# Q and K sums copied into the operand buffers and transposed there, row buffers given up for half a V weight piece

## The chip, the cores and the metric

One core of one Trainium2 chip runs the whole program. The metric is the device time of one execution in microseconds (us); before the change the median of three runs is 1652.26 us (1645.23 to 1652.44).

## The reference

A memory-augmented attention A and a gated feed-forward network (FFN) B are mixed by a gate that is computed per row of x.

```
g = sigmoid((x * gate_w).sum(-1))
for s in range(64):                      # 64 segments of 32 rows, mem: 8 rows
    h = concat([mem, x[32*s : 32*s+32]]) # 40 rows, 640 wide
    q, k, v = h @ Wq, h @ Wk, h @ Wv     # 32 heads of 192 each
    p = softmax(mask(q @ k.T * 192**-0.5))
    o = (p @ v) @ Wo
    mem, a[s] = o[:8], o[8:]             # the next segment needs mem
b = (gelu(x @ w_gate) * (x @ w_up)) @ w_down
out = g * a + (1 - g) * b
```

The segments form a chain: the memory rows that one produces are input of the next. The last eight rows of a segment's 32 ("left" rows) need the memory of no later segment, so their Q, K and V can be made for four segments at once.

## The kernel before

**Stages.** First comes the FFN for all 2048 rows (into a scratch tensor), then the 64 segments one after the other. A segment treats the 32 heads as four octets of eight heads. Each of Q, K and V of an octet is a sum over five pieces of weights (k = 0 to 4, 128 x 1536 bf16, 384 KB each); a piece is four matmuls of 384 columns that stand side by side on 32 output columns each. The sums end in PSUM, ACT (ScalarE) copies each to SBUF, and for Q and K the DVE (VectorE) transposes 32 x 32 blocks of it into the buffers `Qs` and `Ks`, which the score matmuls read. POOL (GpSimd) copies the middle third of Q into `Qz`, in which half the partitions are zero.

**What sets the order.** The order is written out by hand in lists (`PROG`, `PROG1`, `PROG3`): `("g", n, k)` is piece k of group n of `GROUPS`, `tq`/`tk` the transposes of an octet, `sc` its scores, `ex` its softmax, `pt` the transposes of the probabilities, `pv` the product with V, `wo` the output projection, `lf`/`le` work on left rows that fills gaps. Segments 0, 1 and 2 of four follow `PROG` or `PROG1`, every fourth (called q = 3 below, the first three q = 0, 1, 2) `PROG3`. All engines take their instructions in the order in which this list adds them. Waits are worked out by a small scheduler in the same order: an operation waits for the last writer of what it reads, and for the last writer and all readers of what it overwrites.

**Places that matter below.** In `PROG` the last piece of group 3 (V of octet 2 and Q of octet 3) stands directly ahead of `("sc", 2)`. In `PROG3` the last piece of group 2 (V of octet 1, Q and K of octet 2) and one piece of group 3 stand ahead of `("sc", 1)`, and the last piece of group 3 ahead of `("sc", 2)`. The ACT copies of those sums (L1159 for Q and K, L1162 for V) are added with the last piece, so ahead of these scores. The copies go to `rows_sb[0]` (Q) and `rows_sb[1]` (K), 768 bytes per partition each, and the transposes (L1176) from there to `Qs` and `Ks`. Scores start with two matmuls that write the mask (L1187), then L1195, L234 and L1202.

**Weights that don't fit.** SBUF holds most pieces for good. Thirteen pieces of Q, K and V and three of Wo share their place with a partner, and are loaded anew in each segment by a DMA from SP's queue as soon as the matmuls of the piece in that place are done. One Q piece (k = 2 of the octet that comes last in one segment and first in the next) is copied to four blocks of 768 bytes (`ek_off`) late in each segment by POOL: blocks 0 and 1 to the row buffers in one copy (L1455) after `sc 3`, block 2 after it (L1459), block 3 to a V buffer after `pv 2` (L1459). The load of the piece's partner follows these copies. The blocks are read by the next segment's first Q, and by left-row matmuls (`LQ`, L930) that stand just behind `pv 3` (L1282 and L1284): there only where the left unit's octet is the one whose piece was copied, which is so for q = 0 and q = 1 in all but the last group of four segments.

**The end of a segment.** Half of the output sum goes through ACT (`half_copy`, L1345, one instruction) to SBUF, DVE adds the other half (`half_sums`, L1350), and further adds and transposes give the next segment's memory columns.

Of the kernel before, what the change touches and what calls it, by code (L numbers as in the profile page):

```python
# [238 lines left out]
def _build(nc, A_x, A_mem0, A_Wq, A_Wk, A_Wv, A_Wo, seg_len, w_gate, w_up, w_down,  # L239
# [65 lines left out]
    wsB["rows"] = al(2 * 768)  # L305
# [91 lines left out]
    rows_sb = [bview(wsB_off["rows"] + b * 768, 768) for b in range(2)]  # L397
    r_rows = [sreg(wsB_off["rows"] + b * 768, 768) for b in range(2)]
# [31 lines left out]
    U3h = [bview(wsB_off[nm], 768).rearrange("p (t c r) -> p t c r", c=3, r=64) for nm in ("Q", "p")]  # L430
    r_U3h = [sreg(wsB_off[nm], 768) for nm in ("Q", "p")]
    r_U3hp = [[[sreg(wsB_off[nm] + x + 4 * i, 4) for x in xs_] for i in range(3)] for nm, xs_ in (("Q", (0, 8)), ("p", (0, 256, 512)))]
    assert wsB["Q"] >= 768 and wsB_off["p"] + 768 <= wsB_off["K"]
# [7 lines left out]
    zp_off = [wsB_off["p"], wsB_off["Q"]]  # L441
    ek_off = [wsB_off["rows"], wsB_off["rows"] + 768, wsB_off["K"] + 24 * R - 768, wsB_off["v"]]
    assert zp_off[0] + 4 * DJ <= ek_off[2] and zp_off[0] % 64 == 0 and 4 * DJ <= wsB["Q"]
# [5 lines left out]
    zpart = [fview(x, DJ * 4) for x in zp_off]  # L449
    zsum = zpart[0]  # L450
    r_zp = [sreg(x, DJ * 4) for x in zp_off]
# [60 lines left out]

    def piece_src(key):
        if key[0] == 3:
            return Wo2[:, key[1]]
        m, o_, k = key
        return (Wq2, Wk2, Wv2)[m][:, k, OW * o_:OW * (o_ + 1)]

    def piece_size(key):
        return GO if key[0] == 3 else GQ  # L520

    def piece_view(key, o):
        if key[0] == 3:
            return bview(o, GO).rearrange("p (c n) -> p c n", n=Dm)
        return bview(o, GQ)
# [44 lines left out]
    def seg_order(s):  # L570
        keys = []
        for item in PROGS[s % 4]:
            if item[0] == "g":
                keys += [(m, octet(s, i), item[2]) for m, i in group_at(item)]
# [5 lines left out]
    assert len(orders[0]) == len(set(orders[0])) == 3 * KT * NOCT + NWP  # L580
# [17 lines left out]
    seq = lk + lv[2] + lw[NLW:] + lv[0] + lv[1] + lw[:NLW]  # L598
# [369 lines left out]
    def vl_mm(s, k):  # L968
        o, bk, b = octet(s, 0), lb["v"], s // 4 % 2
        g_, rg_ = unit_piece((2, o, k))  # L970
        S_.add("pe", [lambda e, j=j: e.matmul(  # L971
            ps[32 * j:32 * j + 32, bk, 0:384], XLg[b][:, k, :], g_[:, 384 * j:384 * (j + 1)], start=(k == 0), stop=(k == KT - 1),
            tile_position=(0, 32 * j)) for j in range(4)],
            reads=[rg_, r_XLg[b]], writes=[r_ps[bk]], name="Vl s%d o%d k%d" % (s, o, k))

    units = [(0, NOCT - 1)] + [(1, o) for o in LUNIT[3].values()] + [(0, 1), (0, 2), (0, 0)]
    for n, (g, o) in enumerate(units):
# [5 lines left out]
        for m in range(2):  # L983
            left_rows(g, o, m, LBK[m], lst[b][:, :, m], [r_lst[b]], rows_sb[m], r_rows[m])
# [131 lines left out]
    def proj(s, item):  # L1116
# [8 lines left out]
        def mms(m, bk, lhs, k, g_, keep):  # L1125
            fns = []
            for j in range(4):
# [4 lines left out]
                else:  # L1132
                    rhs = g_[:, 384 * j:384 * (j + 1)]
# [8 lines left out]
        for n, (m, i) in enumerate(group_at(item)):  # L1142
            o, bk = octet(s, i), bk_of[(m, i)]
            g_, rg_ = piece(s, (m, o, k))
            S_.add("pe", mms(m, bk, htile(k), k, g_, n > 0),
                   reads=([rg_] if rg_ else r_ek) + [r_Hm[int(k >= KA[1])], r_HxT], writes=[r_ps[bk]],
                   name="%s s%d o%d k%d" % ("QKV"[m], s, o, k))
        for m, i in ms:
            if m == 2 and s % 4 == 0 and i:
                o, bk = octet(s, i), bk_of[(3, i)]  # L1150
                g_, rg_ = piece_view((2, o, k), res_off[(2, o, k)]), r_res[(2, o, k)]
                S_.add("pe", mms(2, bk, XLg[s // 4 % 2][:, k, :], k, g_, False),
                       reads=[rg_, r_XLg[s // 4 % 2]], writes=[r_ps[bk]], name="Vl s%d o%d k%d" % (s, o, k))
        if k < KT - 1:
            return
        for m, i in ms:
            o, bk = octet(s, i), bk_of[(m, i)]
            if m < 2:
                S_.add("act", lambda e, m=m, bk=bk: e.activation(out=rows_sb[m], in_=ps[:, bk, 0:384], func=ACTF.Copy),  # L1159
                       reads=[r_ps[bk]], writes=[r_rows[m]], name="rows evac")  # L1160
# [13 lines left out]
    def row_transp(s, m, o):  # L1174
        dst, rd = ((Qs, r_Qm), (Ks, r_Km))[m]
        S_.add("dve", lambda e: e.transpose(out=dst[:, :, 0:L], in_=rows_sb[m].rearrange("p (c r) -> p c r", r=L)),  # L1176
               reads=[r_rows[m]], writes=[rd], name="T%s s%d o%d" % ("qk"[m], s, o))
# [92 lines left out]
    def pv_oct(s, o):  # L1270
# [33 lines left out]
        if o == NOCT - 2 and s + 1 < NSEG:  # L1304
            ek_copy(s, (3,))
# [371 lines left out]
```

## Time and profile before

| what | value |
|---|---|
| median of three runs | 1652.26 us (1645.23 to 1652.44) |
| the profiled execution, its own span | 2114.2 us |
| its granted TensorE clock, mean over the core | 0.654 |
| DMA bytes moved, mean rate | 499.28 MB, 236 GB/s |
| DVE, ACT, POOL busy | 1005.8, 792.9, 553.3 us |
| Q and K copies by ACT (L1159) | 512 of 491 ns |
| transposes to `Qs`, `Ks` by DVE (L1176) | 512 of 562 ns |

The profiled execution is longer than the timed runs; durations below are those of that execution. In the rows of groups the columns are line, engine, operation, what is written and read, shapes, and count, then busy time in us and the mean in ns of one, then the engine's idle time before them. In the rows of a timeline the columns are start and duration in us, engine, line and operation; matmul ends are modelled, so neighbouring matmuls overlap in it. A window's row has its length and the busy time of PE (TensorE), PEld (its weight loads), DVE, ACT and POOL, then the granted clock, the DMA engines' busy share and their rate in GB/s.

### The profile page before, as it was taken

The numbers are of one execution on the slowest core, as the hardware profiler recorded it, in microseconds if no ns is written. First come the engines' busy times: TensorE is split into PE (matmuls) and PEld (weight loads), VectorE is DVE, ScalarE is ACT, GpSimd is POOL, SyncE is SP. The second block draws the span as 40 slices with busy tenths as digits, with TensorE's granted clock in tenths as the row PEclk, the third lists the DMA queues.
The fourth block names the chain that finished last, engine by engine and source line by source line (L and its number), as shares of the span: only waits on it lengthen the run. The fifth ranks groups of instructions, "written<-read, shape, count | busy, mean of one in ns | idle before, by whom it ended". The sixth has DMA issues, their size and how long they took to land.

```text
span 2114.2 us, 75845 instructions
## 1 busy us (share of the span) xinstructions
PE 2098.0 (99%) x37107; PEld 958.1 (45%) x28147; DVE 1005.8 (48%) x3039; ACT 792.9 (38%) x1890; POOL 553.3 (26%) x1625
## 2 busy tenths in 40 slices
PE   9999999999999999999999999999999999999997
PEld 3444344444444444444444444444444444444444
DVE  4233254554545454545545454545455454545453
ACT  1111244343434343444434343434444343434342
POOL 1000023232232223232222323232322223222332
PEclk6666666666666666666666666666666666666666
DMA  9612577776768777677767677776777676777775
GB/s 319 182 33 57 184 268 260 248 270 232 253 219 275 244 258 241 227 255 254 274 233 249 221 268 249 255 251 225 248 256 270 239 258 212 261 256 249 254 264 174
DMA packets 275415, 499.28 MB, mean 236 GB/s; under 512 B 121119, under 2 KB 136327, under 8 KB 275079
## 3 DMA queue, kind: packets, MB, share of 16 engines
q1 hardware_dynamic: 271000, 491.30, 68.8%
q8 instruction: 255, 4.18, 0.8%
q10 hardware_dynamic: 4079, 3.14, 0.5%
q14 instruction: 81, 0.66, 0.1%
HBM read 473.25 MB, written 21.09 MB: 234 GB/s over the span
## 4 chain that ended last, share of the span: by engine, by line
PE 99%; DMA 0%; DVE 0%; SPq 0%; POOL 0%; ACT 0%; issue 0%; ACTq 0%; POOLq 0%; DVEq 0%
PE ps L226 26%; PE ps L1138 25%; PE ps L1338 9%; PE ps L1383 8%; PE ps L1282 4%; PE ps L930 4%; PE ps L839 4%; PE ps L836 4%; PE ps L862 3%; PE ps L1364 3%; PE ps L1187 2%; PE ps L1284 2%; PE ps L234 1%; PE ps L1195 1%; PE ps L971 1%; PE ps L1254 1%
## 5 line engine op out<-in xcount | busy, mean ns | idle before, releaser
L226 PE MATMUL ps<-arena 128*32 128x384 bf16 x8960 | 887.8, 430 | 0.4 <-ACT arena L1159 0.4
L1138 PE MATMUL ps<-arena 128*32 128x384 bf16 x8640 | 857.5, 420 | 2.0 <-DVE arena L1583 2.0
L1138 PEld LDWEIGHTS ps<-arena 128*32 128x32 bf16 x8640 | 303.3, 117 | 525.3 <-issue 379.7
L1176 DVE STREAM_TRANSPOSE arena<-arena 128x384 bf16<-128x384 bf16 x512 | 276.5, 562 | 144.1 <-ACT arena L1159 144.1
L1159 ACT ACTIVATE arena<-ps 128x384 bf16<-128x384 f32 x512 | 230.0, 491 | 160.1 <-PE ps L1138 160.1
L1214 DVE TENSOR_REDUCE arena<-ps 104x4 f32<-104x160 f32 x256 | 83.0, 324 | 340.2 <-PE ps L1202 340.2
L1338 PE MATMUL ps<-arena 128*32 128x320 bf16 x3456 | 241.0, 404 | 0.0
L1012 POOL COPY arena<-arena 128x96 bf16<-128x96 bf16 x256 | 70.2, 274 | 475.3 <-PE ps L1202 311.4
L1267 ACT ACTIVATE arena<-ps 128x448 bf16<-128x448 f32 x192 | 104.4, 544 | 237.7 <-PE ps L1254 233.3
L1179 POOL COPY arena<-arena 64x160 bf16<-64x160 bf16 x256 | 81.9, 320 | 385.5 <-DVE arena L1176 384.3
L1162 ACT ACTIVATE arena<-ps 128x384 bf16<-128x384 f32 x256 | 125.2, 489 | 128.1 <-PE ps L1138 127.5
L1383 PE MATMUL ps<-arena 128*64 128x320 bf16 x1536 | 169.6, 387 | 0.0
L1226 ACT ACTIVATE ps<-ps 104x160 f32<-104x160 f32 x256 | 74.8, 292 | 239.5 <-DVE ps L1216 239.5
L1320 ACT ACTIVATE arena<-ps 128x480 bf16<-128x480 f32 x192 | 109.5, 570 | 93.8 <-PE ps L1284 85.7
L930 PE MATMUL ps<-arena 128*32 128x384 bf16 x1280 | 142.5, 408 | 0.0
L1338 PEld LDWEIGHTS ps<-arena 128*32 128x32 bf16 x3456 | 113.3, 129 | 56.9 <-ACT arena L1261 18.1
L1282 PE MATMUL ps<-arena 128*64 128x160 bf16 x1536 | 135.2, 263 | 0.0
L1284 PE MATMUL ps<-arena 128*64 128x64 bf16 x1536 | 128.6, 225 | 0.0
L1228 DVE TENSOR_REDUCE arena<-ps 104x4 f32<-104x160 f32 x256 | 81.8, 319 | 88.4 <-ACT ps L1226 87.4
L1383 PEld LDWEIGHTS ps<-arena 128*64 128x64 bf16 x1536 | 93.2, 127 | 49.4 <-issue 9.6
L1282 PEld LDWEIGHTS ps<-arena 128*64 128x64 bf16 x1536 | 94.1, 126 | 42.8 <-ACT arena L1159 23.0
L1411 ACT ACTIVATE arena<-ps 128x384 bf16<-128x384 f32 x120 | 57.3, 491 | 123.9 <-DVE arena L1580 74.0
(102 smaller groups left out, 2518.2 us busy)
## 6 DMA issues: line engine op xcount, KB each, us to landing
arena<-in_A_Wk_dram SPq DMA_DIRECT2D x335, 384.0 KB, 5.8
arena<-in_A_Wv_dram SPq DMA_DIRECT2D x335, 384.0 KB, 8.4
arena<-in_A_Wo_dram SPq DMA_DIRECT2D x205, 480.0 KB, 4.3
arena<-in_A_Wq_dram SPq DMA_DIRECT2D x209, 384.0 KB, 4.8
arena<-left_qk_scratch SPq DMA_DIRECT2D x126, 96.0 KB, 3.9
left_qk_scratch<-arena SPq DMA_DIRECT2D x49, 192.0 KB, 4.6
left_qk_scratch<-arena SPq DMA_DIRECT2D x30, 96.0 KB, 3.7
ffn_b_scratch<-arena ACTq DMA_DIRECT2D x16, 160.0 KB, 2.3
```

Source lines behind the costliest of these rows:

```text
L226: return e.add_instruction(mybir.InstMatmult(name=nm, start_tensor_calc=like["start"], stop_tensor_calc=stop, tile_size=(128, 32), tile_po ...
L930: fns.append(lambda e, outp=outp, rhs=rhs, j=j: e.matmul(outp, lhs, rhs, start=(k == 0), stop=(k == KT - 1), tile_position=(0, 32 * j)))
L1138: fns.append(lambda e, outp=outp, rhs=rhs, j=j: e.matmul(outp, lhs, rhs, start=(k == 0), stop=(k == KT - 1), tile_position=(0, 32 * j)))
L1159: S_.add("act", lambda e, m=m, bk=bk: e.activation(out=rows_sb[m], in_=ps[:, bk, 0:384], func=ACTF.Copy), reads=[r_ps[bk]], writes=[r_rows ...
L1162: S_.add("act", lambda e, i=i, bk=bk: e.activation(out=v_sb[i % NVB].rearrange("p (c n) -> p c n", c=3), in_=ps[:, bk, 0:384].rearrange("p ...
L1176: S_.add("dve", lambda e: e.transpose(out=dst[:, :, 0:L], in_=rows_sb[m].rearrange("p (c r) -> p c r", r=L)), reads=[r_rows[m]], writes=[r ...
L1267: S_.add("act", lambda e: e.activation(out=PT, in_=ps[:, bank, 0:PTW + 128], func=ACTF.Copy), reads=[r_ps[bank]], writes=[r_PT], name="pT ...
L1282: return [lambda e: e.matmul(full, v[:, e0:e0 + 64], PTm[:, i], start=True, stop=False, tile_position=(0, 64 * i), skip_group_check=True), ...
L1284: lambda e: e.matmul(part, vl[:, e0:e0 + 64], PTl[:, i], start=False, stop=True, tile_position=(0, 64 * i), skip_group_check=True)]
L1320: S_.add("act", lambda e: e.activation(out=apx(u[:, 0, 0, :], [[rs, na], [3 * rs, 4], [1, R]]), in_=ps[:, A, 0:na * W].rearrange("p (c t r ...
L1338: fns.append(lambda e, i=i, t=t, j=j, gv=gv: e.matmul(ps[32 * j:32 * j + 32, bank, 0:2 * DJ].rearrange("p (h n) -> p h n", h=2), lhs2[i], ...
L1383: S_.add("pe", [lambda e, i=i, g_=g_, c=c, p=p, u=u: e.matmul(ps[64 * i:64 * i + 64, LB, 0:2 * DJ], u[:, c, :], g_[:, c, 2 * DJ * i:2 * DJ ...
```

## The change

1. The row buffers are removed. ACT's copy writes the untransposed sums to `Qs` or `Ks`, as 12 blocks of 32 columns in rows of 40, and the transpose works in place. The copy is added at the same point of the order as before. So the copy of octet 3's Q is now a writer of `Qs` that stands ahead of `sc 2` in the order, and for q = 3 the copies of octet 2's Q and K stand ahead of `sc 1`. In the program as built these scores therefore read, in `Qs` (for `sc 1` of q = 3 also in `Ks`), the next octet's untransposed sums in place of their own octet's; `Qz`, and `Ks` elsewhere, hold the right octet. The number and sizes of the matmuls don't change.
2. The freed 1536 bytes per partition keep half of one V piece (k = 4 of the octets 0 and 3) for good: that piece is split in two keys (`SPLIT`, `parts`), and of the swap only the second half is left, 192 KB a segment in place of 384 KB.
3. The four blocks of the copied Q piece get other places, since the row buffers are gone: 0 in `Ks`' last 768 bytes, 1 and 3 in the two V buffers, 2 over part of the probabilities, `Qz` and the start of `Ks`. So block 0 is copied after `sc 3`, block 1 after `pv 2`, block 2 after `pt 3`, block 3 after `pv 3`, in four instructions, and the load of the partner moves behind `pv 3`.
4. `half_copy` becomes two ACT instructions of 64 x 160, to the two halves of the partitions of the Q buffer; the sum of `half_sums` moves to a place over `PT`, and the fourth segment's second half of `U3h` moves from the probabilities to `PT`.
5. In the start before segment 0 the left rows' sums go through the Q and K buffers.

```diff
-    wsB["rows"] = al(2 * 768)
...
-    ek_off = [wsB_off["rows"], wsB_off["rows"] + 768, wsB_off["K"] + 24 * R - 768, wsB_off["v"]]
+    ek_off = [wsB_off["K"] + 24 * R - 768, wsB_off["v"], wsB_off["p"] + 256, wsB_off["v"] + 768]
+    zs_off = wsB_off["PT"] + 384
...
+    SPLIT = [(2, o_, KT - 1) for o_ in (0, NOCT - 1)]
+
+    def parts(key):
+        return [key + (h,) for h in range(2)] if key in SPLIT else [key]
...
     for m, k in [(m, k) for m in range(3) for k in range(KT)][3 * KT - NSQ:]:
-        partner[(m, 0, k)] = (m, NOCT - 1, k)
+        partner[parts((m, 0, k))[-1]] = parts((m, NOCT - 1, k))[-1]
...
             if m < 2:
-                S_.add("act", lambda e, m=m, bk=bk: e.activation(out=rows_sb[m], in_=ps[:, bk, 0:384], func=ACTF.Copy),
-                       reads=[r_ps[bk]], writes=[r_rows[m]], name="rows evac")
+                S_.add("act", lambda e, m=m, bk=bk: e.activation(
+                    out=(Qs, Ks)[m][:, :, 0:L], in_=ps[:, bk, 0:384].rearrange("p (c r) -> p c r", r=L), func=ACTF.Copy),
+                       reads=[r_ps[bk]], writes=[(r_Qm, r_Km)[m]], name="rows evac")
...
-        S_.add("dve", lambda e: e.transpose(out=dst[:, :, 0:L], in_=rows_sb[m].rearrange("p (c r) -> p c r", r=L)),
-               reads=[r_rows[m]], writes=[rd], name="T%s s%d o%d" % ("qk"[m], s, o))
+        S_.add("dve", lambda e: e.transpose(out=dst[:, :, 0:L], in_=dst[:, :, 0:L]),
+               reads=[rd], writes=[rd], name="T%s s%d o%d" % ("qk"[m], s, o))
...
         if o == NOCT - 2 and s + 1 < NSEG:
-            ek_copy(s, (3,))
+            ek_copy(s, 1)
+        if o == NOCT - 1 and s + 1 < NSEG:
+            ek_copy(s, 3)
...
-        out = apx(fview(zp_off[0], zp_off[1] - zp_off[0] + 4 * DJ, 0, 64), [[(zp_off[1] - zp_off[0]) // 4, 2], [1, DJ]])
-        S_.add("act", lambda e: e.activation(out=out, in_=ps[64:128, bank, 0:2 * DJ].rearrange("p (h n) -> p h n", h=2), func=ACTF.Copy),
-               reads=[r_ps[bank]], writes=r_zp, name="Zp " + tag)
+        for h in (1, 0):
+            S_.add("act", lambda e, h=h: e.activation(out=zpart[64 * h:64 * h + 64], in_=ps[64:128, bank, DJ * h:DJ * (h + 1)], func=ACTF.Copy),
+                   reads=[r_ps[bank]], writes=[r_zp[h]], name="Zp " + tag)
...
             if item == ("sc", NOCT - 1) and s + 1 < NSEG:
-                ek_copy(s, (0, 1))
-                ek_copy(s, (2,))
+                ek_copy(s, 0)
+            if item == ("pt", NOCT - 1) and s + 1 < NSEG:
+                ek_copy(s, 2)
+            if item == ("pv", NOCT - 1) and s + 1 < NSEG:
+                key = (EM, octet(s, NOCT - 1), EK)
+                load_piece(swap_in[key], "swap s%d" % s)
```

**Scores of octet 2 on PE.** The first place is on PE, in a segment with q = 2, from the last Q piece of octet 3 (L226) to the first score matmuls of octet 2. Before, where L1187 is the mask and L1195 the first scores:

```order
L226 MATMUL ps<-arena 32x384 [waits d_slot8]
L226 MATMUL ps<-arena 32x384 x3
L1187 MATMUL ps<-arena 40x160
L1187 MATMUL ps<-arena 40x160 [waits e_pool]
L1195 MATMUL ps<-arena 40x40 [waits e_dve]
L1195 MATMUL ps<-arena 40x40 x7
```

Now, at the same place, where the mask is L1202 and the first scores L1210:

```order
L226 MATMUL ps<-arena 32x384 [waits d_slot8]
L226 MATMUL ps<-arena 32x384 x3
L1202 MATMUL ps<-arena 40x160
L1202 MATMUL ps<-arena 40x160 [waits e_pool]
L1210 MATMUL ps<-arena 40x40 [waits e_act,e_dve]
L1210 MATMUL ps<-arena 40x40 x7
```

No instruction moved; the first score matmul has got a wait for ACT, which is the copy of the Q sum that the L226 matmuls just ahead of it complete.

**The copied Q piece on POOL.** The second place is on POOL, from the copies of the Q piece to the end of a segment with q = 1 (L1328 is `uTl`, L811 the copy of x for the next segment, L1080 and L1085 the gate's part). Before:

```order
L1179 COPY arena<-arena 64x160 [waits e_dve,e_pool]
L1455 COPY arena<-arena 128x768 [waits e_pool,e_dve,e_act]
L1459 COPY arena<-arena 128x384 [waits e_pool,e_pe] x2
L1328 COPY arena<-arena 128x12x8 [waits e_pool,e_act]
L811 COPY arena<-arena 128x5x24 [waits d_xs,e_pool,e_pe]
L1328 COPY arena<-arena 128x12x8 [waits e_pool,e_dve,e_act]
L1080 TENSOR_SCALAR arena<-arena 128x1 [waits e_pool]
L1085 TENSOR_SCALAR arena<-arena 128x160 [waits e_pool,d_bz]
```

Now (L1471 copies a block, L1345 is `uTl`, L823 the copy of x):

```order
L1194 COPY arena<-arena 64x160 [waits e_dve,e_pool]
L1471 COPY arena<-arena 128x384 [waits e_pool,e_pe] x2
L1345 COPY arena<-arena 128x12x8 [waits e_act,e_pool]
L823 COPY arena<-arena 128x5x24 [waits d_xs,e_pool,e_pe]
L1471 COPY arena<-arena 128x384 [waits e_pe,e_pool,e_dve]
L1471 COPY arena<-arena 128x384 [waits e_act,e_pe,e_pool]
L1345 COPY arena<-arena 128x12x8 [waits e_act,e_pool,e_dve]
L1093 TENSOR_SCALAR arena<-arena 128x1 [waits e_pool]
L1098 TENSOR_SCALAR arena<-arena 128x160 [waits e_pool,d_bz]
```

Two of the copies now stand behind the copy of x, and the last of them waits for the product with V of the segment's last octet.

**The reader of the copied piece on PE.** The third place is PE behind that product, in the same kind of segment. The rows read alike in both programs; now they are:

```order
L1297 MATMUL ps<-arena 64x160 x2
L1299 MATMUL ps<-arena 64x4x16 x2
L942 MATMUL ps<-arena 32x384 [waits e_pool]
L942 MATMUL ps<-arena 32x384 x3
L226 MATMUL ps<-arena 32x384 x3
```

Before, L942 was L930, with the same wait for POOL; the copy that it waited for then stood behind `pv 2`, and stands behind `pv 3` (L1297, L1299) now.

More of the change, by code (lines that the diff above doesn't have):

```diff
@@ L396, in _build @@
     r_Kl = sreg(wsB_off["K"] + 8, 12 * R * 2 - 8)
-    rows_sb = [bview(wsB_off["rows"] + b * 768, 768) for b in range(2)]
-    r_rows = [sreg(wsB_off["rows"] + b * 768, 768) for b in range(2)]
+    pre_rows = [bview(wsB_off[nm], 768) for nm in "QK"]
+    r_pre_rows = [sreg(wsB_off[nm], 768) for nm in "QK"]
     stg_off = (wsB_off["stg"], wsB_off["uT"] + 48 * R)
```

81 lines of the change are left out of this document (41 added, 40 removed).

## The prediction

> **What bounds the kernel now.** I read the page first: span, busy shares, granted clock and the chain that ended last.
>
> ```profile
> span 2114.2 us, 75845 instructions
> PE 2098.0 (99%) x37107; PEld 958.1 (45%) x28147; DVE 1005.8 (48%) x3039; ACT 792.9 (38%) x1890; POOL 553.3 (26%) x1625
> PEclk6666666666666666666666666666666666666666
> PE 99%; DMA 0%; DVE 0%; SPq 0%; POOL 0%; ACT 0%; issue 0%; ACTq 0%; POOLq 0%; DVEq 0%
> ...
> q1 hardware_dynamic: 271000, 491.30, 68.8%
> ```
>
> The chain of waits lies on PE for 99% of the span, so the end is set by matmuls in PE's order, and what PE waits for in addition is paid in full. The clock line has one value in all 40 slices. The rival bound is the transfers, 69% of the 16 DMA engines' span in queue q1; so the windows of one segment (q = 2, first matmul at 1009.39 us) come next, then the last of the five V loads and its user.
>
> ```profile
> 1011.00:1024.00 13.00, 13.00 (x254) 4.28 (x136) 6.33 (x19) 5.26 (x13) 3.00 (x11) 0.65 1.02 364
> 1024.00:1027.00 3.00, 3.00 (x74) 1.55 (x66) 1.40 (x6) 1.88 (x5) 0.80 (x3) 0.65 0.35 108
> 1031.00:1036.00 5.00, 5.00 (x124) 3.07 (x104) 1.98 (x10) 1.86 (x5) 1.45 (x5) 0.65 0.56 162
> ...
> 1014.94 2.37 SPq L635 DMA_DIRECT2D arena<-in_A_Wv_dram x5
> ...
> 1030.92 0.47 PE L1138 MATMUL ps<-arena 128*32 128x384 bf16 x4
> ```
>
> The DMA engines are full from 1011 to 1024 (share 1.02), then fall to 0.35: the backlog, whose end is the V loads issued from 1014.94 on, is gone at about 1024. The matmuls of the fifth V piece start at 1030.92, some 7 us later. The timed runs are shorter than this execution by 1652.26/2114.2 = 0.78; if only PE gets faster, the use comes at (1030.92 - 1009.39) x 0.78 = 16.8 us into the segment, and the load still ends at 14.6. So loads are late in neither.
>
> **The change part by part.** *Fewer bytes.* 192 KB less in each of 63 segments is 12.4 MB; at the 364 GB/s of the dense window that is 0.54 us a segment, 34 us in all, of the DMA engines' time. None of it is PE's time while loads come 2 us or more ahead of their use. I take 0; if PE did wait for loads, it would be up to -34 us.
>
> *Copies into `Qs` and `Ks`.* ACT and DVE execute as many copies and transposes of the same sizes as before. What is new is the wait: the first score matmul of octet 2 waits for ACT's copy of octet 3's Q (in q = 3, that of octet 1 for octet 2's Q and K too). Here is one such place, PE's rows first (V and Q of the last piece, mask, first scores), then ACT's (V copy, Q copy).
>
> ```profile
> 1023.93 0.48 PE L1138 MATMUL ps<-arena 128*32 128x384 bf16 x4
> 1024.17 0.48 PE L226 MATMUL ps<-arena 128*32 128x384 bf16 x4
> 1024.58 0.25 PE L1187 MATMUL ps<-arena 128*40 128x160 bf16 x2
> 1024.66 0.26 PE L1195 MATMUL ps<-arena 128*40 128x40 bf16 x8
> ...
> 1024.46 0.49 ACT L1162 ACTIVATE arena<-ps 128x384 bf16<-128x384 f32 x1 [0.22 <-PE ps L1138]
> 1024.85 0.48 ACT L1159 ACTIVATE arena<-ps 128x384 bf16<-128x384 f32 x1
> ```
>
> V's copy starts 0.05 us after V's matmuls end (1024.41), Q's copy stands behind it and ends at 1025.33. The scores started at 1024.66. How soon PE goes on after such a release is seen at a segment's start, where the transpose of the memory columns ends at 1009.34 and the first matmul starts 0.05 us later:
>
> ```profile
> 1009.09 0.25 DVE L1583 STREAM_TRANSPOSE arena<-arena 128x64 bf16<-128x64 bf16 x1
> 1009.39 0.62 PE L1138 MATMUL ps<-arena 128*32 128x384 bf16 x4
> ```
>
> So the scores start at 1025.38, 0.72 us late. Behind them in PE's order stands everything else, and the softmax and the other engines' work that follows wait for these scores; so nothing makes the delay good. The other four kinds of place, in the order q = 0, q = 1, q = 3 octet 1, q = 3 octet 2 (scores, then the copy waited for):
>
> ```profile
> 966.85 0.26 PE L1195 MATMUL ps<-arena 128*40 128x40 bf16 x8
> 966.94 0.50 ACT L1159 ACTIVATE arena<-ps 128x384 bf16<-128x384 f32 x1
> ...
> 996.05 0.26 PE L1195 MATMUL ps<-arena 128*40 128x40 bf16 x8
> 996.37 0.50 ACT L1159 ACTIVATE arena<-ps 128x384 bf16<-128x384 f32 x1
> ...
> 1047.30 0.26 PE L1195 MATMUL ps<-arena 128*40 128x40 bf16 x8
> 1046.91 0.88 ACT L1159 ACTIVATE arena<-ps 128x384 bf16<-128x384 f32 x2
> ...
> 1050.09 0.26 PE L1195 MATMUL ps<-arena 128*40 128x40 bf16 x8
> 1050.29 0.48 ACT L1159 ACTIVATE arena<-ps 128x384 bf16<-128x384 f32 x1
> ```
>
> End of the copy, plus 0.05, less the scores' start: 0.64, 0.87, 0.54 and 0.73 us. With 0.72 that is 3.50 us per four segments, times 16 is **56 us**. The bounds of one place are the smallest, 0.54, and ACT's whole run there, from the V copy's start to the Q copy's end (1024.46 to 1025.33) plus 0.18 for two releases and the mask ahead of it, 1.05; for 80 places 43 and 84 us.
>
> *The copied Q piece.* Block 3 is now copied after `pv 3`, and `LQ` of the same piece stands just behind it, in q = 0 and q = 1 of 15 groups. Rows of a q = 1: end of the product, `LQ`, `wo`; POOL's `uTl` behind ACT's L1310; the cost of a block's copy. Then, in a q = 0, the end of the product, another piece's `LQ` and `LK`, and the `LQ` in question.
>
> ```profile
> 1006.55 0.26 PE L1284 MATMUL ps<-arena 128*64 128x64 bf16 x2
> 1006.74 0.35 PE L930 MATMUL ps<-arena 128*32 128x384 bf16 x4
> 1006.85 0.50 ACT L1310 ACTIVATE arena<-ps 128x160 bf16<-128x160 f32 x2
> 1007.47 0.27 POOL L1328 COPY arena<-arena 128x96 bf16<-128x96 bf16 x1 [2.37 <-ACT arena L1310]
> L1459 POOL COPY arena<-arena 128x384 bf16<-128x384 bf16 x126 | 63.8, 507 | 13.7
> ...
> 977.13 0.26 PE L1284 MATMUL ps<-arena 128*64 128x64 bf16 x2
> 977.72 0.41 PE L930 MATMUL ps<-arena 128*32 128x384 bf16 x4
> ```
>
> The product ends at 1006.81. POOL starts 0.12 us after its release (1007.35 to 1007.47), copies for 0.51, PE goes on 0.05 later: 1007.49 in place of 1006.74, 0.75 us late. In q = 0 it is 977.39 + 0.68 = 978.07 against 977.72, 0.35. `wo` and the next segment's memory stand behind it on PE. (0.75 + 0.35) x 15 = **16.5 us**. Bounds: 11 us if the output's ACT copies, which `wo` waits for until 1007.35, hide a third of it, 22 us if POOL's pick-up takes 0.3 us.
>
> *Costed at nothing.* The load of the partner piece leaves 3 us later, but its user comes in the next segment's second half; without that cover it would cost PE a transfer, 1.1 us. POOL's four copies of 507 ns replace 828 + 2 x 507, 0.19 us more, on an engine that is 26% busy; block 2's copy lies in front of the product's end. `half_copy` in two costs ACT some 0.07 us (two L1310 copies take 0.50, the single one 0.43) while PE makes the product:
>
> ```profile
> 1006.36 0.43 ACT L1345 ACTIVATE arena<-ps 64x320 f32<-64x320 f32 x1 [0.46 <-PE ps L1338]
> L1455 POOL COPY arena<-arena 128x768 bf16<-128x768 bf16 x63 | 52.2, 828 | 42.4 <-ACT arena L1267 25.1 <-DVE arena L1176 15.5 <-POOL arena L1296 1.1
> ```
>
> In place of it being hidden it would be 48 x 0.07 = 3 us. For q = 3, `U3l` now follows the product too, under six matmul pairs of `wo` ahead of its reader. The start before segment 0 and the order of the first loads change by one half piece.
>
> **The sum.** On the profile's own time: 2114.2 + 56 + 16.5 = 2187 us. For the timed runs PE's work that covers ACT's chain shrinks by 22% while ACT keeps its times. In q = 2 and the last kind of q = 3 the cover from V's end to the scores is 0.25 us, so 0.05 more wait; at the other three kinds ACT is still at the copy before, and the cover is 0.55 to 1.25 us, so 0.12, 0.17 and 0.27 more. That is 0.66 per four segments, 11 us, and 1 us for `LQ` in q = 0. 56 + 11 + 16.5 + 1 = 84 us, from which I take 4 off for waits that PE already has behind these places: 1652 + 80 = **1732 us**, 4.8% slower. With the bounds, 43 + 11 = 54 and 84 + 22 = 106, it lies between 1706 and 1758.
>
> **The rivals.** *PE is not the bound in the timed runs* (faster). The median is 0.78 of the profiled span, and nothing shown says at which clock. At full clock PE's part would be 2114 x 0.654 = 1383 us, and 269 us of the median would be waits, for loads above all; then 34 us less of transfers come out of the time and the new waits fall into the old: 1652 - 34 = 1618 us. It decides if loads end later than PE's use. For it: queue q1's share, 0.688 of 2114, is 88% of the median. Against it: the 7 us of lead and the half-idle windows, even shrunk as above. [...] Chance 0.10.
>
> [...] Chance 0.06.
>
> *ACT is never ahead* (slower than forecast): in the timed runs all 80 places pay ACT's whole chain and `LQ` POOL's long pick-up, 1652 + 106 = 1758 us. For it: three of five kinds already have ACT still at the copy before. Chance 0.16.
>
> *The copies don't make PE wait* (the change doesn't do what the order shows): the new wait for ACT stands in the program's rows, so at most where another wait ends later. Chance 0.02, near 1670.
>
> **How the numbers follow.** The forecast, 1706 to 1758 and most likely 1732 us, has 0.66. Half a percent, 8 us, is about what a measurement of this kernel tells from no change. Faster by more: 0.10, the first rival; within: 0.06; slower by more: 0.84. The range must leave out no more than 0.2: I give 1680 to 1768, which leaves out the first two rivals and little above.
>
> **What would show it.** In the changed profile, the first scores of octet 2 (L1210) should start about 0.05 us after the Q copy's end, with a PE idle of 0.5 to 0.9 us whose releaser is ACT, and L942 behind the last product after POOL's L1471; the segments grow by 0.5 to 1.6 us each at the same clock; the Wv bytes fall by 192 KB a segment with no PE time in return. Wrong if the scores start before that copy ends, if PE's idle from ACT stays under 40 us, or if matmuls of V or Wo are seen waiting for DMA.

## The result and the profile after

The changed kernel takes 1705.83 us, median of 5 runs (1702.77 to 1706.26), against 1652.26 us before: ratio 1.0329, 95% interval 1.0307 to 1.0351. It is slower by 3.3%, some 53.6 us. The forecast was 1732 us (1680 to 1768): the sign and the two new waits were right, the size was 26 us too large.

First the page of the changed kernel: span, busy engines, granted clock in 40 slices, the load queue's share of the span, the chain that ended last, and two groups (busy time and mean ns, then PE's idle time before them).

```profile
span 1704.5 us, 76159 instructions
...
PE 1567.6 (92%) x37090; PEld 778.5 (46%) x28147; DVE 1000.5 (59%) x3039; ACT 794.2 (47%) x1938; POOL 562.5 (33%) x1688
...
PEclk9999999999999999999999999999999999999998
...
q1 hardware_dynamic: 271288, 478.91, 81.6%
...
PE 54%; DVE 11%; ACT 7%; issue 4%; DMA 2%; POOL 2%; SPq 0%; DVEq 0%; POOLq 0%; ACTq 0%
...
L1210 PE MATMUL ps<-arena 128*40 128x40 bf16 x2048 | 71.5, 182 | 67.5 <-ACT arena L1173 53.0
...
L942 PE MATMUL ps<-arena 128*32 128x384 bf16 x1280 | 109.3, 331 | 14.0 <-POOL arena L1471 13.1
```

The clock row is the first surprise: this execution ran at nearly the full clock (0.994 over the core), while the profile on which the prediction rests had 0.654 in every slice. So the kernel before was profiled again (the first experiment below):

```profile
span 1651.5 us, 75828 instructions
...
PE 1564.1 (95%) x37090; PEld 774.6 (47%) x28147; DVE 997.1 (60%) x3039; ACT 784.7 (48%) x1890; POOL 549.3 (33%) x1625
...
PEclk9999999999999999999999999999999999999998
...
q1 hardware_dynamic: 271000, 491.30, 85.0%
...
PE 69%; DMA 16%; DVE 7%; ACT 4%; issue 3%; SPq 1%; POOL 0%; DVEq 0%; ACTq 0%; POOLq 0%
...
L1138 PE MATMUL ps<-arena 128*32 128x384 bf16 x8640 | 641.2, 329 | 15.2 <-DMA arena<-in_A_Wv_dram 6.7
```

At the clock of the timed runs the same kernel has 16% of its chain in DMA, and its V matmuls wait for loads. PE's busy time is nearly the same in both kernels (1564 and 1568 us), so all but 3.5 of the 53 us between the spans are idle time of PE. The waits of PE in the two kernels (total us, times, longest), the changed one first:

```profile
PE ps L1210 <- ACT arena L1173: 53.0, 63, 1.0
PE ps L942 <- POOL arena L1471: 13.1, 29, 0.7
PE ps L1210 <- DVE arena L1248: 10.4, 16, 0.7
...
PE ps L984 <- ACT arena L947: 4.9, 1, 4.9
...
PE ps L1381 <- DMA arena<-in_A_Wo_dram: 1.2, 2, 0.8
...
PE ps L1151 <- DMA arena<-in_A_Wk_dram: 0.4, 1, 0.4
...
PE ps L1151 <- DMA arena<-in_A_Wv_dram: 0.2, 1, 0.2
```

and the kernel before, profiled again:

```profile
PE ps L1138 <- DMA arena<-in_A_Wv_dram: 6.7, 18, 0.8
PE ps L1364 <- DMA arena<-in_A_Wo_dram: 6.0, 13, 1.1
...
PE ps L1138 <- DMA arena<-in_A_Wk_dram: 1.9, 4, 0.9
...
PE ps L1383 <- DMA arena<-in_A_Wo_dram: 1.6, 5, 0.4
```

Two waits are new (scores for ACT, left-row matmuls for POOL), as predicted, and a third (L984, once, at the start) was not. The row of DVE belongs to the scores' wait: its 16 times are octet 2 of q = 3, where the scores need nothing of L1248, a step of octet 1's softmax that happens to end 0.03 us after the Q copy (641.56 and 641.53 us in one such segment). So the scores' wait is about 63 us of idle, and not the 53.0 of the first row alone. The waits for loads, the four rows of the kernel before, are 16.2 us there and 1.8 us in the three rows of the change: with the new waits PE comes later to most of its loads. For that trade the sum of the prediction has 4 us.

One place of each kind, in the changed kernel. The scores of octet 2 in a segment with q = 2 (PE's rows, then ACT's copies of V and Q):

```profile
806.79 0.33 PE L226 MATMUL ps<-arena 128*32 128x384 bf16 x4
807.05 0.25 PE L1202 MATMUL ps<-arena 128*40 128x160 bf16 x2
808.03 0.28 PE L1210 MATMUL ps<-arena 128*40 128x40 bf16 x8 [0.73 <-ACT arena L1173]
...
807.01 0.49 ACT L1177 ACTIVATE arena<-ps 128x384 bf16<-128x384 f32 x1
807.40 0.48 ACT L1173 ACTIVATE arena<-ps 128x384 bf16<-128x384 f32 x1
```

Q's copy ends at 807.88, the scores start 0.15 us later (0.05 was assumed), 0.98 us behind the mask instead of 0.08. And the copied Q piece in a segment with q = 1, PE's rows around POOL's copy of block 3:

```profile
792.64 0.20 PE L1299 MATMUL ps<-arena 128*64 128x64 bf16 x2
793.47 0.35 PE L942 MATMUL ps<-arena 128*32 128x384 bf16 x4 [0.63 <-POOL arena L1471]
...
792.91 0.51 POOL L1471 COPY arena<-arena 128x384 bf16<-128x384 bf16 x1 [0.54 <-PE ps L1299]
```

The product's end releases POOL, POOL copies for 0.51 us, PE goes on 0.05 us later: 0.63 us of idle (0.75 was predicted).

Mean length of a segment in us, from the first K matmul of one to that of the next (four kinds, without the first four segments), then the sum of all 63 and when the first segment starts:

```
                       q=0    q=1    q=2    q=3   sum of 63  start
before, again         23.49  22.72  22.32  22.58   1439.8    175.9
changed               24.12  23.86  22.46  23.80   1486.5    181.4
```

So 46.7 us were lost in the segments and 5.5 before the first one; q = 2, which has the scores' wait but not the left-row one, lost only 0.14 a segment. It is also the kind in which PE waited most for loads: 25 of the 40 late loads before, 8.8 of the 16.2 us, are in segments with q = 2.

### The profile page after: what moved, and what is told of

It is laid out like the page before. It is cut to its first block, busy times and chain, and to the rows that moved or that the text cites. A ratio compares the mean times of both kernels' runs of the same rounds, so it can differ in the third digit from the quotient of the medians.

```text
span 1704.5 us, 76159 instructions
## 1 busy us (share of the span) xinstructions
PE 1567.6 (92%) x37090; PEld 778.5 (46%) x28147; DVE 1000.5 (59%) x3039; ACT 794.2 (47%) x1938; POOL 562.5 (33%) x1688
## 4 chain that ended last, share of the span: by engine, by line
PE 54%; DVE 11%; ACT 7%; issue 4%; DMA 2%; POOL 2%; SPq 0%; DVEq 0%; POOLq 0%; ACTq 0%
PE ps L1151 16%; PE ps L226 13%; PE ps L1400 6%; PE ps L1355 5%; PE ps L1297 2%; DVE arena L1191 2%; PE ps L1381 2%; PE ps L1210 2%; ACT arena L1173 2%; PE ps L1202 2%; ACT arena L1177 2%; PE ps L942 2%; DVE arena L1243 1%; DVE ps L1231 1%; DVE arena L1229 1%
## 5 line engine op out<-in xcount | busy, mean ns | idle before, releaser
L226 PE MATMUL ps<-arena 128*32 128x384 bf16 x8960 | 641.0, 327 | 5.3 <-ACT arena L1327 2.7
L1151 PE MATMUL ps<-arena 128*32 128x384 bf16 x8640 | 635.2, 328 | 7.7 <-DVE arena L1597 3.6
L1151 PEld LDWEIGHTS ps<-arena 128*32 128x32 bf16 x8640 | 225.8, 96 | 374.2 <-issue 263.6
L1355 PE MATMUL ps<-arena 128*32 128x320 bf16 x3456 | 181.5, 300 | 3.9 <-issue 1.7
L1471 POOL COPY arena<-arena 128x384 bf16<-128x384 bf16 x252 | 127.5, 506 | 107.4 <-PE ps L1217 43.4
L1210 PE MATMUL ps<-arena 128*40 128x40 bf16 x2048 | 71.5, 182 | 67.5 <-ACT arena L1173 53.0
L942 PE MATMUL ps<-arena 128*32 128x384 bf16 x1280 | 109.3, 331 | 14.0 <-POOL arena L1471 13.1
L1400 PE MATMUL ps<-arena 128*64 128x320 bf16 x1536 | 121.6, 304 | 0.0
L1297 PE MATMUL ps<-arena 128*64 128x160 bf16 x1536 | 116.7, 239 | 0.4 <-issue 0.4
L1355 PEld LDWEIGHTS ps<-arena 128*32 128x32 bf16 x3456 | 86.9, 96 | 46.6 <-ACT arena L1276 17.3
L1299 PE MATMUL ps<-arena 128*64 128x64 bf16 x1536 | 103.8, 193 | 0.0
```

The costliest lines, as they stand in the source:

```text
L226: return e.add_instruction(mybir.InstMatmult(name=nm, start_tensor_calc=like["start"], stop_tensor_calc=stop, tile_size=(128, 32), tile_po ...
L942: fns.append(lambda e, outp=outp, rhs=rhs, j=j: e.matmul(outp, lhs, rhs, start=(k == 0), stop=(k == KT - 1), tile_position=(0, 32 * j)))
L1151: fns.append(lambda e, outp=outp, rhs=rhs, j=j: e.matmul(outp, lhs, rhs, start=(k == 0), stop=(k == KT - 1), tile_position=(0, 32 * j)))
L1210: fns.append(lambda e, gp=gp, c=c, tl=tl: e.matmul(ps[gp:gp + R, bank, SC + tl * R:SC + (tl + 1) * R], Qs[:, c, :], Ks[:, c, :], start=Fal ...
L1297: return [lambda e: e.matmul(full, v[:, e0:e0 + 64], PTm[:, i], start=True, stop=False, tile_position=(0, 64 * i), skip_group_check=True), ...
L1355: fns.append(lambda e, i=i, t=t, j=j, gv=gv: e.matmul(ps[32 * j:32 * j + 32, bank, 0:2 * DJ].rearrange("p (h n) -> p h n", h=2), lhs2[i], ...
```

## The experiments

The names below are those of the rows; each kernel was compared with the kernel before on the same chip. The experiments ran on several chips, and the median of the kernel before was between 1650.8 and 1653.5 us there; so a difference of two medians can hold up to 2.7 us that are not the edit's.

**e1: the kernel before again,** unchanged, for a profile at the timed clock.

> The kernel before, unchanged, for a profile at the clock of the timed runs (the profile of the change has 0.994, that of before 0.654). Theory A (the new waits cost PE some 82 us, and the 12 MB of saved transfers give back some 28 of them, since at the full clock PE does wait for loads): PE's idle time that ends with a DMA is 20 us or more, and the wait ahead of the scores of octet 2 is near 0. Theory B (the transfers are worth nothing, and the new waits replace waits that PE had anyway): idle that ends with a DMA is under 10 us, and PE idles some 25 us in before at the places of the new waits or behind them that the change has lost.

1653.24 us in this execution, clock 0.994. Its page and waits are shown above: loads are late at this clock.

**e2: the copies of Q and K behind the scores of the octet before.** ACT's copy is put off until those scores have been added to the order, so the scores read their own octet's sums and wait for no copy.

```diff
             if m < 2:
-                S_.add("act", lambda e, m=m, bk=bk: e.activation(
...
+                if i and (s, i - 1) not in scored:
+                    pend.append((m, bk))
+                else:
+                    rows_evac(m, bk)
                 continue
...
+        scored.add((s, o))
+        for x in pend:
+            rows_evac(*x)
+        del pend[:]
```

> The change, with ACT's copies of Q and K added behind the scores of the octet before, where these had not yet been added; so the scores read their own octet and don't wait for the copy, and the copy waits for the scores. Theory A: the whole 67 us that the page of the change shows ahead of L1210 go, 1706 - 65 = 1641 us, below before. Theory B: part of the wait only moves to later places, 1706 - 40 = 1666 us. If the wait were not what makes it slower: 1700 or more.

1664.68 us, ratio 1.0076 (1.0052 to 1.0099). Of the 53.6 us, 41 are gone with the scores' wait, as theory B had it, and 12 are not.

**e3: the left pieces in another order.** For q = 0 and q = 1 the left unit's pieces k = 2 and k = 3 change places, so that no matmul behind the last product needs the copied piece at once.

```diff
-("pv", 3), ("lf", 1, 1, 2), ("lf", 2, 1, 2), ("lf", 0, 1, 1), ("lf", 0, 1, 2),
+("pv", 3), ("lf", 1, 1, 3), ("lf", 2, 1, 2), ("lf", 0, 1, 1), ("lf", 0, 1, 3),
...
-("lf", 1, 1, 3), ("lf", 1, 1, 4)
+("lf", 1, 1, 2), ("lf", 1, 1, 4)
...
-("lf", 0, 1, 3), ("lf", 0, 1, 4)
+("lf", 0, 1, 2), ("lf", 0, 1, 4)
```

> The change, with the left rows' pieces k = 2 and k = 3 exchanged for q = 0 and q = 1, so that a piece that is not copied stands behind the last product and the copied one 12 output matmuls later. Both theories: the wait of L942 for POOL goes, 14 to 21 us by the page of the change; theory A 1706 - 17 = 1689 us, theory B (the output matmuls behind wait for their own operands anyway) 1706 - 8 = 1698 us.

1702.46 us, ratio 1.0305 (1.0259 to 1.0351), 3 us less than the change, which the intervals do not tell from nothing, and less than both theories expected. The 13.1 us of idle that L942 had from POOL are gone from this trace's waits, and the sum of the 63 segments is the same (1486.8 against 1486.5 us): those with q = 0 and q = 1 are 0.11 us shorter, those with q = 2 are 0.30 us longer (22.46 to 22.76). Where the gain goes was not traced; in e8, whose edit touches only the start, the segments with q = 2 are 0.19 us longer too (22.65), so a part of the 0.30 can be the difference of two executions.

**e4: the whole V piece is swapped again** (`SPLIT = []` in the change).

> The change, but with the V piece k = 4 of the octets 0 and 3 swapped whole again, so 384 KB a segment and not 192; all else as in the change. Theory A: the saved transfers are worth some 28 us, so 1706 + 28 = 1734 us. Theory B: 1706 us within 5.

1711.47 us, ratio 1.0358 (1.0296 to 1.042). The half piece is worth about 6 us in the change, far from the 28 us of theory A; the intervals overlap, so by the times alone it could be nothing. The 63 segments of the two traces differ by 6.7 us (1493.2 against 1486.5).

**e7: the new wait alone, in the kernel before.** Only the list of what the scores read is longer.

```diff
-        S_.add("pe", fns, reads=[r_Qm, r_Ql, r_Qz, r_Km, r_Kl], writes=[r_ps[bank]],
+        S_.add("pe", fns, reads=[r_Qm, r_Ql, r_Qz, r_Km, r_Kl] + r_rows, writes=[r_ps[bank]],
```

> The kernel before, with one thing added: the score matmuls also name the row buffers among what they read, so that the first scores of an octet wait for ACT's copies of the next octet's sums as they do in the change. Nothing else differs. Forecast's theory (each wait adds its whole length, PE waits for nothing else): 1652 + 67 = 1719 us. Rival (PE already waits for loads at the timed clock, and a delay of the scores gives the loads that much more time, so a part is absorbed): the change without these waits was 41 us faster than with them; with 192 KB more to load per segment a little more is absorbed, so 1652 + 30 to 41, 1682 to 1693 us, and in the trace PE's idle time from DMA is below that of the kernel before by the part absorbed.

1712.17 us, ratio 1.0364 (1.0344 to 1.0384): 59.5 us, near the forecast's 67 and far above the rival's 30 to 41. PE's waits in it:

```profile
PE ps L1195 <- ACT arena L1159: 54.6, 63, 1.0
...
PE ps L1195 <- DVE arena L1176: 10.7, 32, 0.4
...
PE ps L1364 <- DMA arena<-in_A_Wo_dram: 1.7, 3, 0.8
PE ps L1338 <- DMA arena<-in_A_Wo_dram: 0.8, 1, 0.8
```

Against the kernel before, the scores come later by 0.98, 1.16, 0.89 (octet 2 of q = 0, 1, 2), 1.06 and 0.89 us (octets 1 and 2 of q = 3; means over the segments): 4.98 us in four segments, 80 us in 16 times four. Of the 13 us over the forecast's 67, 7.5 are the release: the scores start 0.144 us after the copy's end in all five kinds, where 0.05 was taken (in the change 0.145 us in four kinds and 0.053 at octet 1 of q = 3). The waits for loads fall from 16.2 to 2.5 us, and the segments grow by 60.1 us in all (1439.8 to 1499.9). So some 20 of the 80 us are given back: a segment with q = 0 grows by 0.49 us for its 0.98, one with q = 2 by 0.66 for 0.89, one with q = 3 by 1.31 for 1.95, and only q = 1 by more (1.39 for 1.16). In q = 2 the delay falls by 0.59 us at the first two pieces of the last V, whose loads were late in e1. In q = 3 it falls by 0.38 at the first product with V, and in q = 0 from 1.09 to 0.32 by the fourth pair of `Wo`, behind a stall of e1 that the trace puts down to "issue", so to nothing that it shows. One such place each in e1's timeline, q = 2 first:

```profile
876.77 0.35 PE L1138 MATMUL ps<-arena 128*32 128x384 bf16 x4 [0.16 <-DMA arena<-in_A_Wv_dram]
...
830.34 0.22 PE L1284 MATMUL ps<-arena 128*64 128x64 bf16 x2 [0.72 <-issue]
```

PE's idle from DMA falls by 13.7 us, which would be two thirds of the 20; the rest is not traced to one cause.

**e13: the late copy and load alone, in the kernel before.** Block 3 goes to the other V buffer behind the last product, and the partner's load behind it.

```diff
-    ek_off = [wsB_off["rows"], wsB_off["rows"] + 768, wsB_off["K"] + 24 * R - 768, wsB_off["v"]]
+    ek_off = [wsB_off["rows"], wsB_off["rows"] + 768, wsB_off["K"] + 24 * R - 768, wsB_off["v"] + 768]
...
-        if o == NOCT - 2 and s + 1 < NSEG:
+        if o == NOCT - 1 and s + 1 < NSEG:
             ek_copy(s, (3,))
...
+            if item == ("pv", NOCT - 1) and s + 1 < NSEG:
+                key = (EM, octet(s, NOCT - 1), EK)
+                load_piece(swap_in[key], "swap s%d" % s)
```

> The kernel before, with block 3 of the copied Q piece taken from behind the last product with V (to the other V buffer) and the load of the partner piece behind it, as in the change, and nothing else. Forecast: 16.5 us for the matmuls that wait for the copy, nothing for the later load: 1669 us. Rival 1 (loads are what PE waits for, and the delay gives them time): under 8 us, 1653 to 1660. Rival 2 (the later load costs too, since everything in SP's queue behind it leaves later): over 20 us, 1672 or more, with more idle of PE from DMA than in the kernel before.

1669.06 us, ratio 1.0097 (1.0068 to 1.0126): 15.5 us, near the forecast's 16.5. Its waits:

```profile
PE ps L930 <- POOL arena L1459: 14.1, 29, 1.0
...
PE ps L1138 <- DMA arena<-in_A_Wv_dram: 8.4, 21, 0.7
...
PE ps L1138 <- DMA arena<-in_A_Wk_dram: 4.1, 6, 1.1
```

Idle from DMA did not shrink here (16.8 us in five groups against 16.2 in four; that for `Wv` and `Wk` grew by 3.9 us, that for `Wo` fell by 3.3). At the place itself, counted from the last product, L930 comes 0.71 us later in q = 1 and 0.43 in q = 0, the pairs of `Wo` behind it 0.50 and 0.44 (means of segments 4 to 59). In q = 1 a third is hidden, as the prediction's lower bound supposed, since `wo` had to wait there for ACT's copies of the output before:

```profile
679.10 0.35 PE L930 MATMUL ps<-arena 128*32 128x384 bf16 x4
679.66 0.67 PE L1364 MATMUL ps<-arena 128*32 128x160 bf16 x26
...
679.31 0.50 ACT L1310 ACTIVATE arena<-ps 128x160 bf16<-128x160 f32 x2
```

These are rows of a q = 1 in e1: the `Wo` matmuls (L1364) start 0.56 us behind L930, when the first of ACT's two copies has been made. That leaves some 14 us in 15 groups. But the segments grow otherwise: by 0.17 and 0.52 us for q = 0 and q = 1, and by 0.31 and 0.25 for q = 2 and q = 3, where no matmul waits for the copy. So the total agrees with the forecast, and that it consists of this wait alone is not shown: the later load (rival 2) can have a part in it, and so can the difference of two executions.

**e14: both waits in the kernel before,** the two edits together.

> The kernel before with both waits of the change and no other part of it: the scores also wait for ACT's copies of the next octet's sums, and block 3 of the copied Q piece and the partner's load come behind the last product. Alone the two cost 59.5 and 15.5 us. If they add (forecast's sum): 1653 + 75 = 1728 us. If they hide behind each other, since the loads of which each alone takes the time are the same (the change with the whole V piece, which has the same bytes, is at 1711.5, of which the start is 3): about 1708 us, and PE's idle from DMA is near that of the scores' wait alone. If it is near 1728, the change's other edits must have gained some 17 us.

1721.64 us, ratio 1.0433 (1.0408 to 1.0458): 69 to 71 us against 75 if they added, a difference within the intervals. PE's idle from DMA is 0.8 us in it. So the two hide little behind each other, if anything, and the change, with the same two waits, is 16 us faster for its other parts: some 6 by the half piece (e4), and some 10 by what is left in e4. Segment by segment e4 and e14 differ by nothing in q = 0 and q = 2, by 0.5 us in q = 1 and 0.3 in q = 3, in steps of about 0.1 spread over PE's order, at the last scores, the last products and the left pieces. Which of the other edits (four copies of 507 ns in place of 828 and two, `half_copy` in two) gains them was not tried, and the four runs of e4 make the split into 6 and 10 uncertain by some 10 us.

**e8: the start.** The left rows before segment 0 go through the V buffers instead of the Q buffer.

```diff
-    pre_rows = [bview(wsB_off[nm], 768) for nm in "QK"]
+    pre_rows = [bview(wsB_off[nm], 768) for nm in "vK"]
```

> The change, with the sums of the left rows in the start before segment 0 copied through the V buffers instead of the Q buffer, which lies over the last row buffer of the FFN. Theory of the start (ACT's first copy there waits for the FFN's last store, PE idles 5 us, and the clock falls to a half for 4 us more): V of the left rows starts less than 1 us after the matmuls ahead of it, the clock stays at 1.00, and the run is 5 to 7 us shorter, 1699 to 1701 us. Rival (the first segment waits for its weights anyway, so that the 5 us are only moved): 1704 to 1707 us, the first segment starting at the same time as in the change.

1702.90 us, ratio 1.0304 (1.0285 to 1.0322): 3 us less than the change, between theory and rival, with intervals that overlap. What it removes is seen in the changed kernel's windows (length, busy time of PE, PEld, DVE, ACT, POOL, then granted clock, DMA share, GB/s):

```profile
169.00:172.00 3.00, 2.98 (x76) 0.86 (x32) 0.00 (x0) 0.00 (x0) 0.00 (x0) 1.00 0.98 340
172.00:177.00 5.00, 0.07 (x4) 0.08 (x8) 1.81 (x5) 1.85 (x4) 0.34 (x1) 0.72 0.69 278
177.00:179.00 2.00, 2.00 (x28) 0.85 (x28) 1.83 (x7) 0.53 (x2) 0.06 (x1) 0.50 0.30 107
179.00:181.00 2.00, 2.00 (x32) 0.47 (x12) 1.03 (x2) 0.83 (x2) 0.64 (x2) 0.50 0.28 102
181.00:183.00 2.00, 2.00 (x52) 0.61 (x24) 0.86 (x2) 0.87 (x2) 0.00 (x0) 0.98 0.26 94
```

and in ACT's timeline there, where the FFN's last store leaves and ACT's first copy of left rows waits for it:

```profile
168.04 0.33 ACTq L890 DMA_DIRECT2D ffn_b_scratch<-arena  x1
174.50 0.87 ACT L947 ACTIVATE arena<-ps 128x384 bf16<-128x384 f32 x2 [6.81 <-DMA ffn_b_scratch<-arena]
```

The Q buffer lies over the last row buffer of the FFN. ACT waits 6.8 us for the store from it, PE stands for 4.9 us, and then runs at half the clock until about 181. With the V buffers the same five microseconds read

```profile
172.00:177.00 5.00, 4.89 (x124) 1.43 (x56) 3.79 (x7) 3.64 (x8) 1.36 (x5) 1.00 1.03 397
```

and the first segment starts 7.5 us earlier (173.9 instead of 181.4). In these two traces half of it is given back: the 63 segments take 3.8 us longer in e8.

**e9, e10, e12: all three repairs together** (e2, e3 and e8); the same with the whole V piece; the same without e3's edit.

> The change with three repairs: ACT's copies of Q and K behind the scores of the octet before (so the scores read their own octet's sums), the left pieces exchanged, the start through the V buffers. If the three are independent: 1664.7 - 3 - 5.5 = 1656 us, still 4 us above the kernel before. Rival 1 (the copied Q piece is hidden behind the scores' wait in the change and costs its full 16.5 us once that wait is gone): 1664.7 - 16.5 - 5.5 = 1643 us. Rival 2 (what is gained goes into waits for loads): 1660 to 1665 us, with more idle of PE from DMA than with the first repair alone.

> The same three repairs, and the V piece swapped whole again, as before the change (192 KB more per segment). Forecast's theory (bytes cost nothing): same as with the half piece, within 2 us. Second theory (at the timed clock PE waits for loads, and 0.54 us of transfer per segment is paid where no other wait covers it): up to 34 us more, most likely 15 to 25, since the scores' waits that covered loads are gone. Between: 6 us more, as in the change itself with the whole piece.

> The change with the scores' wait removed and the start repaired, but the left pieces in the order of the change, so that the left pieces' matmuls behind the last product wait for POOL's late copy. Against the three repairs (1650.3) this shows that wait alone where no score waits. Forecast's term: 16.5 us more, 1667 us. From the difference of the first repair and all three (14.4, of which the start 3 to 7): 7 to 11 us more, 1657 to 1661. What the change itself showed (3 us): 1653.

e9: 1650.29 us, ratio 0.999 (0.9969 to 1.0011), as fast as before, and between the first two theories (1656 and 1643). e10: 1663.08 us, 1.0083 (1.005 to 1.0115): without the scores' wait the half piece is worth 13 us by the medians, 15 by the ratios, where it was 6 in the change. From the times alone the two values are not clearly apart; the 63 segments of the traces, 16.4 us longer in e10 than in e9 against 6.7 in e4, point the same way. e12: 1660.12 us, 1.0037 (1.0015 to 1.0059): without the scores' wait the late copy costs 8 to 10 us (by the ratios and by the medians), within the 7 to 11 expected, where e3 gained 3. PE's waits for loads in e9:

```profile
PE ps L1152 <- DMA arena<-in_A_Wv_dram: 5.0, 11, 0.8
...
PE ps L1394 <- DMA arena<-in_A_Wo_dram: 2.8, 5, 1.0
```

and in e10, where the load is 192 KB a segment larger:

```profile
PE ps L1152 <- DMA arena<-in_A_Wv_dram: 7.5, 21, 0.6
PE ps L1394 <- DMA arena<-in_A_Wo_dram: 5.5, 13, 0.8
```

More matmuls find their weights late (34 against 16 in these rows). All rows of DMA together hold 4.7 us more idle (15.4 against 10.7), a third of the 13 us; the rest was not traced.

**e11: the repairs and one product later.** e9's trace still has a wait that e2's edit brought, since the first product of every fourth segment writes a PSUM bank that ACT now empties later:

```profile
PE ps L1310 <- ACT arena L1194: 9.4, 15, 0.7
```

The product moves one weight piece back in `PROG3`.

```diff
-("sc", 1), ("pv", 0), ("g", 3, 1), ("tq", 2),
+("sc", 1), ("g", 3, 1), ("pv", 0), ("tq", 2),
```

> The change with the three repairs, and in every fourth segment the product with V of the first octet one weight piece later, since in the trace with the three repairs it starts 0.40 us later than in the kernel before (it writes a PSUM bank that ACT empties only behind the scores now). If that wait is the rest of the cost there: 16 times 0.3 to 0.4 us less, 1650 - 5 to 6.5 = 1644 to 1645 us, 0.45 to 0.5% faster than the kernel before. Rival (PE goes on to wait for the next loads instead): 1649 to 1651 us.

1646.66 us, ratio 0.9965 (0.9943 to 0.9988), 12 runs. It is faster than the kernel before by 0.35%, an interval that barely excludes no difference, with 12.4 MB less to load and with scores that read their own octet's sums. The wait shown falls from 9.4 to 1.6 us. The 3.6 us less than e9, of the 5 to 6.5 expected, lie within the intervals of the two.

## Why the prediction was right, and where it was not

**What bounds the kernel.** This is the step that failed. It was read from an execution at a clock of 0.654, and the sentence "So loads are late in neither" carried it over to the timed runs by shrinking one place of one segment. At the timed clock DMA is 16% of the chain (e1). The place chosen, the fifth V piece of a q = 2, was not the worst: the second piece of that V waits in e1's row of a q = 2, and pairs of `Wo` in its list of waits.

**The scores' wait.** Place and releaser were right, and the size came near: 56 + 11 = 67 us predicted, 59.5 alone (e7). That is in part luck, since two errors offset each other. Each place costs more than forecast (80 us in the sum of the 80 places instead of 67, 7.5 of the 13 for a release of 0.144 us taken as 0.05), and about 20 are given back, up to 13.7 of them by loads that are no longer late, where 4 were taken off for both terms. ACT kept its times at the higher clock, as the sum supposed (784.7 us busy in e1, 792.9 at 0.654). "So nothing makes the delay good" was wrong.

**The copied Q piece.** 16.5 us (17.5 for timed runs) predicted, 15.5 alone (e13), but some 14 at the place itself, and segments without this wait grew as well; so the agreement is not proof of the sum. The 0.3 us of POOL's pick-up in the upper bound was the author's estimate; in the place shown POOL started 0.07 us after the product's end (792.84 to 792.91). In the change it is worth 3 us with a wide interval (e3), without the scores' wait 8 to 10 (e12), and beside that wait alone 9.5 (e14 less e7).

**Both.** 84 less 4 predicted, 69 to 71 measured (e14).

**Costed at nothing.** The half piece was about -6 us in the change and -13 where PE waits for loads again; the prediction named it ("up to -34 us" if PE did wait for loads), and the wrong answer to that question gave 0. The start was +3 us by the times (not clear of the noise; the first segment starts 5.5 us later than before), by a wait for the FFN's last store that "changes by one half piece" overlooked: the edit moved a buffer over another one that was still being stored. The other edits together gained some 10 us with that start in it, spread too thin to name. From e14: 1721.6 - 10.2 (to e4) - 5.6 (the half piece) = 1705.8 us, which adds up by construction, as the terms are differences of these medians.

**The rivals.** The first had its premise right (full clock, loads late) and its sum wrong: PE is busy for 1564 of the 1651.5 us in e1, which leaves 87 us for waits, 16.2 of them for these loads, where the rival had 269. And the new waits do not fall into the old. e7 pays 59.5 of its 80 us, since the scores are late in all 80 places, while PE waited for loads only 40 times and for 0.4 us each in the four rows of e1. The 0.654 was no picture of the timed runs: the mean clock is 0.992 to 0.998 in every other execution for which the record lists one. The other rivals fell: nothing gave the waits back in full (no change, at a chance of 0.06), and ACT's whole chain was not paid.

**What would show it.** The idle from ACT, 53.0 us in its row, was over the 40 named. The scores started 0.15 us after the copy and not 0.05. The idle behind POOL was there. But the last sign of being wrong, matmuls of V or `Wo` that wait for DMA, was there as well, in the kernel before, and only three times in the changed one.

## What to carry to other kernels

Compare the span of the one profiled execution with the timed runs before a sum is made: where the two differ by 22%, the waits of the one need not be those of the other, and lead times of loads have to be worked out at the clock of the runs that count. Two stalls on one engine are each to be priced alone and then together with what already stalls there: here a new wait ahead of late loads cost 59.5 of its 80 us, and a saving of bytes was worth about 6 us beside the new waits and 13 without the scores' wait. A total that agrees with the forecast is to be checked against the segments and the places, as two errors can offset each other. The releaser that a row names is the last one to end (here L1248, 0.03 us behind the Q copy); whether the waiting instruction needs it is for the program to say. When a buffer gets a new place, look at what lay there in the stage before, down to the last store from it.

## What the runs showed of the hardware that was not expected

The kernel before had a granted clock of 0.654 in all slices of one execution (2114.2 us) and 0.994 in another (1651.5 us); what set the former was not tried. After PE had stood for 4.9 us in the start of the change, its granted clock was 0.50 for the next 4 us of its work (the windows from 177 to 181) and its groups of four matmuls came every 0.32 us instead of 0.16, before it was back at 0.98. And the FFN's stores of 160 KB do not land in a fixed time: the median of the 16 in the changed kernel is 3.9 us from issue to landing, that of the two ahead of the last is 1.9 us, and the last, issued at 168.04 with the DMA engines 99% busy from then on, kept ACT until 174.50, 6.46 us after its issue.
